# Four column tiles of a projection as seven half-size products, and the looks at an output matrix moved one stage earlier

## The chip, the cores and the metric

The kernel runs on one core of one Trainium2 chip. The metric is the device time of one execution in microseconds; lower is better. The time before is 679.76 us, the median of 3 runs (679.46 to 680.37). The engines are named as in the profile: PE multiplies matrices, PEld loads its stationary operand, ACT applies functions and copies, DVE does elementwise work, POOL helps a little, and SP issues nearly all transfers from one queue.

## The reference

Two branches read the same `x` (2048 positions, 1024 channels) and are mixed by a gate per position:

```python
g = sigmoid((x * gate_w).sum(-1, keepdims=True))
# branch A: attention over a window of 8 positions, 2 apart, 32 heads of 32
qkv = x @ wqkv;  o = window_attention(q, k, v);  a = o @ wo
# branch B: a gated MLP that mixes positions
z  = gelu(x @ w_in)                       # 2048 x 3584
z1 = z[..., :1792];  z2 = layernorm(z[..., 1792:])
gm = w_sp @ z2 + b_sp[:, None]            # 2048 x 2048 times 2048 x 1792
b  = (z1 * gm) @ w_out
out = g * a + (1 - g) * b
```

Inputs and output are bf16; sums are kept in float32.

## The kernel before

The work on PE goes in stages, one after another. The order on every engine is the order in which the program writes it.

1. z2, first column group (512 columns of `x @ w_in`), positions on the partitions.
2. The projection `x @ wqkv`, in chunks of four blocks of 128 columns. The last two chunks are done as "row pairs" (`row_pair`, line 636): two rows of blocks by two columns of blocks by two halves of the 1024 channels, with seven products in place of eight. This needs sums of blocks of x (`x_sums`, `a22s`, held in z2's later place) and sums of blocks of the weights (`t_w`, `t3_w`). To keep the 16-bit sums accurate, x and the weights are scaled by a power of two first (`whole_power`, line 496), and the results are scaled back when they leave PSUM.
3. z2, the remaining columns: group 1 for positions blocks 2 to 15 (14 tiles), then groups 2 and 3 for all 16 blocks (`z2_tile`, line 291). ACT applies gelu and keeps a sum; after every block of groups 2 and 3 it also squares the whole row of 1792 for the variance (line 760).
4. z1: 14 column tiles of 128 columns (f = 0 to 13), four products of 512 positions each (loop at line 798). ACT applies gelu; the tiles go to a scratch tensor `z1_d`.
5. The spatial product with `w_sp`: two chunks plainly (`g_chunk`, line 822), the other two as seven products (`seven_products`, line 922).
6. The output: w_out and wo, in pairs of rows (`mix_pair`, `both_pairs`, line 1129).

The window attention runs on DVE meanwhile, from stage 2 into stage 5, as a list of steps (`attention_steps`, line 419). ACT does its exponential (line 381) and, when two groups of heads are stored, eight abs-sums of 512 columns (line 415).

A planner places the side work. `Beat` (line 230) holds a clock `beat.now` that advances by 1/2360 us for each column that PE is given. `beat.at(t, fn)` writes `fn` into the program as soon as the clock has passed `t`; attention steps are written when their planned start on DVE is less than `lead` ahead (3 us, in the row pairs 1 us with the large steps halved, `fine`). The clock decides the place of an instruction in its queue, not when it runs: each queue runs in order as its waits allow.

All results of PE go through one pool of PSUM tiles with eight slots (line 79): a product must wait when all eight hold results that nobody has read yet.

Behind the row pairs SP gets a fixed list of loads: w_in for groups 2 and 3 of z2 (line 746), the column of gate_w into the same buffer (line 747), a part of z2 kept aside (line 748), w_in for z1 (`load_w1`, line 488), and a part of the bias (line 752).

Before w_out and wo are multiplied as sums, their largest absolute values are needed. These "looks" (loop at line 773) load two blocks of 128 rows at a time (512 KB) into one of two slots, and ACT sums the absolute values (line 779): seven looks for w_out, four for wo, one every 7 us in stage 4, the sum 11 us behind its load in the planner's clock.

## Time and profile before

| | us |
|---|---|
| median of 3 runs | 679.76 |
| the profiled execution | 679.49 |
| its span | 677.7 |
| PE busy | 673.0 |
| DVE busy | 558.4 |
| ACT busy | 415.8 |
| the projection ends, z2's stretch begins | 196.28 |
| z2 ends, z1 begins | 262.45 |
| z1 ends, g_chunk begins | 359.14 |
| seven_products begins | 455.83 |
| last product of PE begins | 673.23 |

The granted TensorE clock was 1.00 of full speed. In the profile a row of the timeline gives start, duration, engine, line and operation, and in brackets how long the engine had been idle before it and what released it. "SPq" is SP's queue of transfers, where a row's start is the time of issue. The chain of waits names, step by step, the work that set the end.

### The profile page before, as it was taken

The page shows a single profiled execution, that of the slowest core. Times are in us where ns is not written, and L with a number is a line of the kernel's source. Part 1 is how long each engine was busy: PE and PEld are TensorE (multiplying, and loading weights), DVE is VectorE, ACT ScalarE, POOL GpSimd, SP SyncE. Part 2 cuts the span into 40 slices and gives each one's busy share as a digit, 9 for nine tenths or more (in the row PEclk, how much of TensorE's full clock was granted, in tenths as well). Part 3 has the DMA queues.
Part 4 walks back from the last instruction along what each step waited for, and adds up shares of the span by engine and source line. Part 5 has one row for each costly group of instructions (what it writes and reads, how often), then busy time and mean ns, then how long its engine had stood idle before and what let it go on. Part 6 is the DMA issues. An engine that isn't in the chain of part 4 may idle for free.

```text
span 677.7 us, 8946 instructions
## 1 busy us (share of the span) xinstructions
PE 673.0 (99%) x3311; PEld 355.1 (52%) x3311; DVE 558.4 (82%) x667; ACT 415.8 (61%) x765; POOL 29.4 (4%) x62
## 2 busy tenths in 40 slices
PE   9999999999999999999999999999999999999997
PEld 4499666666654555444444444444444444444443
DVE  4769779999999999999999889974578888766653
ACT  4369676655584999775765996437877542332332
POOL 1000010000000032000010001000000001000000
PEclk9999999999999999999999999999999999999999
DMA  9992977636667416799879997036211513222210
GB/s 231 194 167 61 223 179 224 152 71 175 167 159 213 150 61 164 156 266 350 281 254 227 267 218 183 0 94 233 78 50 44 156 37 88 65 69 68 65 45 32
DMA packets 183192, 100.28 MB, mean 148 GB/s; under 512 B 143342, under 2 KB 169708, under 8 KB 182892
## 3 DMA queue, kind: packets, MB, share of 16 engines
q1 hardware_dynamic: 182316, 97.61, 55.6%
q10 hardware_dynamic: 576, 2.10, 1.0%
q8 instruction: 26, 0.43, 0.3%
q14 instruction: 18, 0.15, 0.1%
q0 software_dynamic: 256, 0.00, 0.0%
HBM read 55.91 MB, written 29.16 MB: 126 GB/s over the span
## 4 chain that ended last, share of the span: by engine, by line
PE 99%; DMA 1%; SPq 0%; ACT 0%; DVE 0%; issue 0%; DVEq 0%
PE ps L621 16%; PE ps L300 14%; PE ps L836 14%; PE ps L809 14%; PE ps L1038 12%; PE ps L910 12%; PE ps L644 7%; PE ps L1127 6%; PE ps L1117 1%; DMA arena<-in_B_w_in_dram 1%; SPq L514 0%; ACT arena L1181 0%; DVE arena L1107 0%; DVEq L1314 0%
## 5 line engine op out<-in xcount | busy, mean ns | idle before, releaser
L621 PE MATMUL ps<-arena 128*128 128x512 bf16 (+1 forms) x640 | 115.1, 336 | 0.0
L300 PE MATMUL ps<-arena 128*128 128x512 bf16 (+1 forms) x512 | 97.9, 353 | 0.5 <-DMA arena<-in_B_w_in_dram 0.5
L621 PEld LDWEIGHTS <-arena 128*128 128x128 bf16 x640 | 83.4, 144 | 27.7
L836 PE MATMUL ps<-arena 128*128 128x512 bf16 x448 | 96.9, 379 | 0.0
L809 PE MATMUL ps<-arena 128*128 128x512 bf16 x448 | 96.9, 379 | 0.0
L1038 PE MATMUL ps<-arena 128*128 128x512 f16 (+1 forms) x392 | 92.8, 379 | 0.0
L910 PE MATMUL ps<-arena 128*128 128x512 bf16 (+1 forms) x392 | 84.8, 379 | 0.0
L300 PEld LDWEIGHTS <-arena 128*128 128x128 bf16 x512 | 50.1, 98 | 47.7 <-DVE arena L320 0.6
L836 PEld LDWEIGHTS <-arena 128*128 128x128 bf16 x448 | 43.9, 98 | 52.8
L809 PEld LDWEIGHTS <-arena 128*128 128x128 bf16 x448 | 43.8, 98 | 52.6
L351 DVE TENSOR_TENSOR arena<-arena 128x8192 bf16<-128x8192 bf16 (+1 forms) x20 | 71.1, 3567 | 0.3
L394 DVE TENSOR_TENSOR arena<-arena,att_A 128x8192 bf16<-128x8192 bf16 (+1 forms) x20 | 71.2, 3564 | 0.0
L1038 PEld LDWEIGHTS <-arena 128*128 128x128 f16 (+1 forms) x392 | 38.4, 98 | 46.2
L910 PEld LDWEIGHTS <-arena 128*128 128x128 bf16 (+1 forms) x392 | 38.3, 98 | 46.3
L354 DVE TENSOR_TENSOR arena<-arena 128x4096 bf16<-128x4096 bf16 (+1 forms) x32 | 56.2, 1756 | 0.8
L305 ACT ACTIVATE arena<-ps 128x512 bf16<-128x512 f32 x64 | 34.2, 536 | 31.2 <-PE ps L300 31.2
L644 PE MATMUL ps<-arena 128*128 128x512 f16 (+1 forms) x224 | 52.4, 379 | 0.0
L630 ACT CAST arena<-ps 128x512 bf16<-128x512 f32 (+1 forms) x64 | 33.1, 561 | 28.4 <-PE ps L621 28.4
L1127 PE MATMUL ps<-arena 128*128 128x512 f16 (+3 forms) x200 | 50.3, 375 | 0.0
L1107 DVE SCALAR_TENSOR_TENSOR arena<-ps,g_s,arena 128x512 bf16<-128x512 f32 (+2 forms) x33 | 24.0, 733 | 29.5 <-ACT arena L1159 20.0
L644 PEld LDWEIGHTS <-arena 128*128 128x128 f16 (+1 forms) x224 | 32.2, 144 | 16.1
L812 ACT ACTIVATE arena<-ps 128x512 bf16<-128x512 f32 x56 | 30.8, 595 | 10.6 <-PE ps L809 10.2
(187 smaller groups left out, 785.4 us busy)
## 6 DMA issues: line engine op xcount, KB each, us to landing
arena<-v_d SPq DMA_DIRECT2D x8, 960.0 KB, 5.1
arena<-k_d SPq DMA_DIRECT2D x7, 960.0 KB, 5.9
arena<-in_A_wqkv_dram SPq DMA_DIRECT2D x24, 256.0 KB, 4.4
z_d<-arena SPq DMA_DIRECT2D x12, 512.0 KB, 8.8
o_d<-arena SPq DMA_DIRECT2D x4, 1024.0 KB
arena<-in_B_w_in_dram SPq DMA_DIRECT2D x4, 1024.0 KB, 9.0
arena<-z_d SPq DMA_DIRECT2D x15, 256.0 KB, 4.8
out_dram<-arena SPq DMA_DIRECT2D x15, 256.0 KB, 2.2
```

The lines of the kernel that those rows point to most:

```text
L300: nc.tensor.matmul(ps[:, 0:N], xT[:, kt, i * P:(i + 1) * P], w2[c][:, kt, 0:N], start=(kt == 0), stop=(kt == KT - 1))
L305: nc.scalar.activation(z2[:, 4 * c:4 * c + n // P, i, :], ps[:, 0:n].rearrange("p (f q) -> p f q", q=P), ACT.Gelu_apprx_tanh, accum_out=s1 ...
L351: TT(prod.rearrange("p (w j c) -> p w j c", w=W, j=8, c=C)[:, w0:w1], in0, in1, ALU.mult)
L354: return lambda: TT(pv[:, :, 0:half], pv[:, :, 0:half], pv[:, :, half:2 * half], ALU.add)
L394: TT(prod.rearrange("p (w j d h) -> p w j d h", w=W, j=8, d=DH, h=HG)[:, w0:w1], in0, in1, ALU.mult)
L621: nc.tensor.matmul(ps[:, n0:n1].rearrange("p (t c) -> p t c", c=C), lhsT, wgt[:, pos0:pos1, kt, :], start=(kt == 0), stop=(kt == KT - 1))
L644: nc.tensor.matmul(dst[:].rearrange("p (t c) -> p t c", c=C), lhs(k), rhs[:, :, k, :], start=first and k == 0, stop=k == 3, skip_group_che ...
L809: nc.tensor.matmul(ps[:], w1[:, kt, (f % 4) * P:(f % 4 + 1) * P], xT[:, kt, 512 * c:512 * (c + 1)], start=(kt == 0), stop=(kt == KT - 1))
L836: nc.tensor.matmul(ps[:], z2[:, f, i, :], wsp[:, i, :, :].rearrange("p a t -> p (a t)"), start=False, stop=(i == 15), skip_group_check=True)
L910: nc.tensor.matmul(dst[:], lhs[:, k, :], rhs(k), start=False, stop=k == 7, skip_group_check=True)
L1038: nc.tensor.matmul(dst[:], lhs[:, j, :], rhs(j), start=first and j == 0, stop=j == 6, skip_group_check=not first)
L1127: nc.tensor.matmul(dst, lhs[:, k, :], rhs[:, k, :], start=first and k == 0, stop=k == 3, skip_group_check=not first)
```

## The change

The first four column tiles of z1 (512 columns of w_in) leave stage 4. They are computed right behind the row pairs, from the sums of x that are still there, in four sets (`ZSet`): each set is one pair of column tiles by 512 positions of even and 512 of odd number, seven products of four matmuls each. The weights are the stationary operand here, x and its sums the moving one; in products one and four x is read at every second element. Each set copies partial results between PSUM tiles on ACT, adds on DVE, applies gelu on ACT with every second element written, and the second set of each column pair stores two tiles to `z1_d`. z1's loop now runs over f = 4 to 13.

What goes with it:

- The 512 columns of w_in are loaded during the projection into the place of group 1 of z2's weights (`z_w`); ACT takes their absolute sums and scales them, DVE forms four sums of weights. z2's group 1 is therefore loaded a second time, and groups 1 and 2 change places.
- The staging of the row pairs goes from four pairs of buffers to three.
- The tile of group 1 for position block 2 is computed inside the last set.
- Behind the sets SP's list is: w1 of chunk 2, w2 of groups 2 and 3, gate_w's column, the part of z2, the bias. w1 of chunk 0 is no longer loaded; chunks 1 and 3 come later.
- Four of the eleven looks move into z2's stretch, into the place of `z_w`, each as two transfers of 256 KB, the first due at once and its abs-sum 9 us later, one every 5.5 us; the sum is written in place. The other seven stay in z1's stage, 7 us apart.
- `scale_sp(2)` moves from DVE to ACT; the load of w_out's first part and the scalings and sums of w_out are moved some places later in `seven_products`.
- In the last pair of rows the final 512 columns are split 256 and 256 in place of 384 and 128, and ACT's scaling ahead of it is split in two.

```diff
+    z_w = w2[1]
+    z_w16 = reg(CD_OFF, KT * 2 * ZC).bitcast(F16).rearrange("p (k c) -> p k c", k=KT)
+    t_z = [z_w16[:, 4:8, 0:256], z_w16[:, 4:8, 256:512],
+           reg(CD_OFF + 16384, 1024).bitcast(F16).rearrange("p (k c) -> p k c", k=4), z_w16[:, 0:4, 768:1024]]
+    odd_f32 = [reg(off, 1024).bitcast(F32) for off in (CD_OFF + 17408, EF_OFF + 14336)]
+    z1p_slots = [reg(off, 4096).rearrange("p (f t) -> p f t", f=2) for off in (EF_OFF + 8192, EF_OFF + 4096)]
...
+    first_looks = [w2_01[:, 4 * r:4 * r + 4, ZC:2 * ZC] for r in range(2)]
...
+    class ZSet:
+        def __init__(self, n):
+            self.r, self.v = divmod(n, 2)
+            self.e5, self.odd = e5_f32[self.v], odd_f32[self.v]
+
+        def mm(self, dst, w, x, first):
+            w = w[:, :, 128 * self.r:128 * self.r + 128]
+            for k in range(4):
+                nc.tensor.matmul(dst[:], w[:, k, :], x[:, k, 512 * self.v:512 * self.v + 512],
+                                 start=first and k == 0, stop=k == 3, skip_group_check=not first)
+            beat.run(4 * 512)
+
+        def bank(self):
+            return psum.tile([P, 512], F32, name="ps", tag="ps")
+
+        def gelu(self, h, odd, src, by):
+            t0 = 1024 * self.v + odd
+            nc.scalar.activation(z1p_slots[self.r][:, h, t0:t0 + 1023:2], src, ACT.Gelu_apprx_tanh, scale=by)
+
+        def one(self):
+            self.pa = self.bank()
+            self.mm(self.pa, z11, x_block(0, 0), True)
+            self.pb = self.bank()
+            nc.scalar.activation(self.pb[:], self.pa[:], ACT.Copy, scale=x_by)
+
+        def two(self):
+            pe = self.bank()
+            self.mm(pe, t_z[0], x_sums[0], True)
+            nc.scalar.activation(self.e5, pe[:], ACT.Copy, scale=z_backs[:, 1:2])
+
+        def three(self):
+            self.mm(self.pb, t_z[1], x_sums[1], False)
+            self.pc = self.bank()
+            nc.scalar.copy(self.pc[:], self.pb[:])
+
+        def four(self):
+            self.mm(self.pa, z21, x_block(1, 0), False)
+            self.gelu(0, 0, self.pa[:], z_backs[:, 0:1])
+
+        def five(self):
+            self.mm(self.pb, t_z[3], x_sums[2], False)
+            self.pd = self.bank()
+            nc.scalar.copy(self.pd[:], self.pb[:])
+            nc.vector.scalar_tensor_tensor(self.odd, self.pb[:], z_backs[:, 1:2], self.e5, ALU.mult, ALU.add)
+            beat.on_vector(0.75)
+
+        def six(self):
+            self.mm(self.pc, z22, x_sums[3], False)
+            nc.vector.scalar_tensor_tensor(self.e5, self.pc[:], z_backs[:, 1:2], self.e5, ALU.mult, ALU.add)
+            beat.on_vector(0.75)
+
+        def seven(self):
+            self.mm(self.pd, t_z[2], a22s, False)
+            self.gelu(0, 1, self.pd[:], z_backs[:, 1:2])
+
+        def rest(self):
+            self.gelu(1, 1, self.odd, 1.0)
+            self.gelu(1, 0, self.e5, 1.0)
+            if self.v:
+                for h in range(2):
+                    f = self.r + 2 * h
+                    sync.dma_start(z1_d[:, :, f * 512:(f + 1) * 512].rearrange("c p t -> p c t"),
+                                   z1p_slots[self.r][:, h, :].rearrange("p (c t) -> p c t", c=4))
...
+    load_w2(1)
+    z_sum(3)
+    for z in z_sets[0:1]:
+        z.two()
+        z.three()
+        z.four()
+    send()
+    for z, z_next in zip(z_sets, z_sets[1:]):
+        z.five()
+        z_next.one()
+        z_next.two()
+        z.six()
+        z_next.three()
+        z.seven()
+        z_next.four()
+        z.rest()
+    z_sets[3].five()
+    ps_2 = psum.tile([P, 512], F32, name="ps", tag="ps")
+    for kt in range(KT):
+        z2_mm(ps_2, 2, 1, kt, ZC)
+    beat.run(KT * ZC)
+    z_sets[3].six()
+    z_sets[3].seven()
+    z_sets[3].rest()
     beat.lead = LEAD
     beat.fine = False
-    for c in (2, 3):
-        sync.dma_start(w2[c][:, :, 0:ZW[c]], win_v[:, :, FH + ZC * c:FH + ZC * c + ZW[c]])
+    load_w1(2)
+    load_w2(2)
+    load_w2(3)
     sync.dma_start(w2[3][:, :, 256:257], gw_v)
     sync.dma_start(z2[:, 4:8, 0:2, :], z2_d[:])
-
-    load_w1(0)
-    load_w1(1)
     sync.dma_start(b_in[:], bass.AP(tensor=B_b_sp.tensor, offset=B_b_sp.offset + 1024, ap=[[1, P], [P, 8]]))
-    for i in range(2, 16):
+
+    wout_v = B_w_out.rearrange("(f p) n -> p f n", p=P)
+    wo_rows = A_wo.rearrange("(k p) n -> p k n", p=P)
+
+    def look(k, t, slot):
+        src = wout_v[:, 2 * k:2 * k + 2, :] if k < 7 else wo_rows[:, 2 * k - 14:2 * k - 12, :]
+        total = w_l1[:, k:k + 1] if k < 7 else wo_l1[:, k - 7:k - 6]
+        for f in range(2):
+            beat.at(t, lambda f=f: sync.dma_start(slot[:, 2 * f:2 * f + 2, :], src[:, f, :].rearrange("p (h c) -> p h c", h=2)))
+        beat.at(t + 9.0, lambda: nc.scalar.activation(slot, slot, ACT.Abs, accum_out=total))
+
+    for k in range(4):
+        look(k, beat.now - 1.0 + 5.5 * k, first_looks[k % 2])
+    for g in range(NG):
+        beat.at(beat.now + 5.0 + 7.0 * g, lambda g=g: turn_wo(g))
+    z2_out(ps_2, 2, 1)
+    for i in range(3, 16):
         z2_tile(i, 1)
-        if i == 3:
-            send()
+        if i == 8:
+            load_w1(1)
...
-    for k in range(11):
-        slot = look_slots[k % 2]
-        src = wout_v[:, 2 * k:2 * k + 2, :] if k < 7 else wo_rows[:, 2 * k - 14:2 * k - 12, :]
-        total = w_l1[:, k:k + 1] if k < 7 else wo_l1[:, k - 7:k - 6]
-        beat.at(beat.now + 2.0 + 7.0 * k, lambda src=src, slot=slot: sync.dma_start(
-            slot.rearrange("p (f n) -> p f n", f=2), src))
-        beat.at(beat.now + 13.0 + 7.0 * k, lambda total=total, slot=slot: nc.scalar.activation(
-            look_out, slot, ACT.Abs, accum_out=total))
...
+    for k in range(4, 11):
+        look(k, beat.now + 2.0 + 7.0 * (k - 4), look_slots[k % 2])
...
-    for f in range(NF):
+    for f in range(4, NF):
```

93 lines of the change are left out of this document (64 added, 29 removed).

## Prediction

> **What bounds the kernel now.** I read the page's parts on engines and on the chain that ended last first, then the chain in order of time.
>
> ```profile
> span 677.7 us, 8946 instructions
> PE 673.0 (99%) x3311; PEld 355.1 (52%) x3311; DVE 558.4 (82%) x667; ACT 415.8 (61%) x765; POOL 29.4 (4%) x62
> ...
> PE 99%; DMA 1%; SPq 0%; ACT 0%; DVE 0%; issue 0%; DVEq 0%
> ...
> 195.42 0.86 PE ps L644 x4
> 196.28 66.16 PE ps L300 x368
> 262.45 96.69 PE ps L809 x448
> ```
>
> PE is busy 673.0 of 677.7 us and is 99% of the chain: the end is set by the number of products. The chain's steps join without a gap: z2's 368 matmuls end at 262.44, where z1's begin, and z1 takes 96.69/448 = 0.216 us for a matmul of 512 columns. A matmul taken away is worth 0.216 us, as long as PE keeps having a free PSUM slot and its operands. So the second reading is of ACT, which empties PSUM in the stretch that the change fills.
>
> ```profile
> 220.50:262.40 41.90, 41.90 (x257) 25.04 (x256) 39.81 (x45) 40.80 (x100) 8.69 (x7) 1.00 0.29 99
> 255.98 0.58 ACT L305 ACTIVATE arena<-ps 128x512 bf16<-128x512 f32 x1
> 257.05 1.70 ACT L760 ACTIVATE arena<-arena 128x1792 bf16<-128x1792 bf16 x1
> 258.74 0.58 ACT L305 ACTIVATE arena<-ps 128x512 bf16<-128x512 f32 x1
> 267.03 0.58 ACT L305 ACTIVATE arena<-ps 128x512 bf16<-128x512 f32 x1
> ```
>
> The row by stage gives ACT 40.80 of 41.90 us in z2's groups 2 and 3, and the timeline of ACT shows it saturated: one block (two gelus and the square) takes 258.74 - 255.98 = 2.76 us, while PE needs 512 + 257 columns x 8 = 2.62 us for it. ACT falls back; the last block's first gelu begins at 267.03, 5.5 us after its product. Eight slots cover that (seven further tiles are 9.2 us), so nothing is lost today. But ACT has no room there.
>
> **The change, term by term.** The sum starts from the profiled execution's own 679.49 us (0.27 below the median; 1.8 us of it lie outside the span).
>
> *Products.* Four column tiles cost 4 x 4 x 8 = 128 matmuls; four sets cost 4 x 7 x 4 = 112. 16 x 0.216 = -3.46 us. z2's tiles stay 14 in number. Bounds on the pace:
>
> ```profile
> L621 PEld LDWEIGHTS <-arena 128*128 128x128 bf16 x640 | 83.4, 144 | 27.7
> L300 PEld LDWEIGHTS <-arena 128*128 128x128 bf16 x512 | 50.1, 98 | 47.7 <-DVE arena L320 0.6
> ```
>
> The only strided operands on PE today are stationary: the projection's weight load with a stride of 16 elements takes 144 ns, a contiguous one 98, +46 ns for 128 columns, and both hide behind 216 ns. The sets read x at every second element as moving operand in 4 x 8 = 32 matmuls. If that cost what the wide stride costs, 4 x 46 = 0.18 us each, it would be +5.9 us; at the other end nothing. I take nothing, since a stride of two is nearer to contiguous than to sixteen. The Trainium skill, "SBUF — State Buffer", section "Door 1: The DMA port swizzle (why `[64,N]` ≈ `[32,N]`)", says that SBUF is read by lines of 16 bytes and that strides are free while several hits fall on a line; two-byte elements at every second place give four hits, so by it the price is nothing, and the 144 ns rows, where each element has its own line, agree with it.
>
> *The sets themselves.* A set is 28 matmuls, 6.05 us of PE, and holds eight ACT operations.
>
> ```profile
> L415 ACT ACTIVATE arena<-arena 128x512 bf16<-128x512 bf16 x32 | 20.0, 624 | 0.1
> L662 ACT ACTIVATE ps<-ps,x_up 128x512 f32<-128x512 f32 x8 | 5.3, 660 | 0.9 <-PE ps L644 0.3
> L556 ACT ACTIVATE arena<-arena,x_up 128x4096 bf16<-128x4096 bf16 x1 | 3.7, 3722 | 0.0
> 193.05 1.73 PE ps L644 x8
> 197.22 0.74 DVE L677 SCALAR_TENSOR_TENSOR arena<-ps,u_l,arena 128x512 bf16<-128x512 f32 x1
> 197.88 0.74 DVE L680 SCALAR_TENSOR_TENSOR arena<-ps,u_l,arena 128x512 bf16<-128x512 f32 x1
> ```
>
> Until the copy for which set 1's third product waits, ACT has eight operations at about 0.6 each (a copy from PSUM is 0.66), the gelu table's load (1.28, a row below) and about four abs-sums of stored attention (0.62): 8.1 to 8.6 us against nine products, 7.8 us. That is a wait of 0.3 to 0.8 us. Later sets hang on DVE: a gelu waits for an addition there, and behind it on ACT's queue stands the copy for the next set but one. In the row pairs the last such product ended at 193.05 + 1.73 = 194.78 and its addition began at 197.88, 3.1 us late; 3.1 + 0.74 + gelu 0.6 + two copies 1.2 = 5.6 us fit into the 6.05 us there are. The gelus write every second element, which no row shows; reading so costs ACT nothing (L556, 3722 ns for 4096 elements, the pace of its contiguous rows), and I take the same for writing. Were it twice the time, 16 x 0.6 = 9.6 us more of ACT in 24 us that are four fifths full already would cost PE up to some 5 us. Together +0.6 us, between 0 and 5.
>
> *The weights' preparation* (1 MB loaded, four abs-sums and four scalings of 1024 on ACT, a small chain on DVE and POOL) lies beside the projection and is due 25 us later: 0. The second load of group 1 (1 MB) has the sets' 25 us as cover: 0; without the cover it would cost about 9 us. Staging with three pairs leaves a pair's stores two pairs, 15 us, to land: 0; were they late, ACT's and DVE's writes would wait first.
>
> *SP's queue behind the sets.* This is the term that decides. T is the end of the last set: 195.42 plus 124 matmuls, 222.2 us.
>
> ```profile
> 198.23 1.17 SPq L746 DMA_DIRECT2D arena<-in_B_w_in_dram  x2
> 206.78 0.37 SPq L747 DMA_DIRECT2D arena<-in_gate_w_dram  x1
> 207.86 1.35 SPq L488 DMA_DIRECT2D arena<-in_B_w_in_dram  x2
> 210.92 4.06 SPq L602 DMA_DIRECT2D k_d<-arena  x1
> ...
> SPq L747 <- DMA arena<-in_B_w_in_dram: 7.3, 1, 7.3
> ```
>
> SP issues in order, and the gate column (L747) waits for the landing of the load before it into the same buffer: 7.3 us today, 206.78 - 198.23 = 8.6 us behind the issue of 1.5 MB. The looks stand behind this wait in the changed order. What is ahead: the last store of z1 waits for a gelu that waits for DVE (3.1 + 0.74 + 0.6 behind the sixth product, which ends 0.9 before T), so it goes out at about T + 4; then w1 and w2, in all 0.5 + 1 + 1 + 0.5 MB.
>
> ```profile
> 198.00:202.00 4.00, 4.00 (x21) 1.81 (x19) 3.96 (x3) 3.56 (x11) 0.00 (x0) 1.00 0.99 205
> 207.90:213.00 5.10, 5.10 (x26) 2.30 (x24) 5.07 (x2) 2.06 (x6) 0.00 (x0) 1.00 0.91 266
> ...
> arena<-in_A_wqkv_dram SPq DMA_DIRECT2D x24, 256.0 KB, 4.4
> ```
>
> While such loads ran, 205 and 266 GB/s were moved; at the mean of 235, 3.15 million bytes take 13.4 us: the gate column is released at about T + 18. Then 210.92 - 206.78 - 1.35 = 2.8 us of issues (column, z2's part, bias), and 4.4 us for a transfer of 256 KB to land: the first look's data arrive at X = T + 25. (Ends: 21, with the higher rate and an early store; 29, at the 8.6 us per 1.5 MB.) The Trainium skill, "DMA: Bandwidth & Descriptors", section "Measured (HBM→SBUF, 128 partitions, SWDGE, issued from GpSimd)", gives 6.15 us for 1 MB; by it 3 MB take 9.2 us and X would be about T + 21, an estimate from that page which the 8.6 us for 1.5 MB here do not support.
>
> *ACT behind the first look.* Its abs-sum is due at T + 8, behind the fifth tile, and in ACT's queue every later gelu stands behind it.
>
> ```profile
> L779 ACT ACTIVATE arena<-arena 128x2048 bf16<-128x2048 bf16 x11 | 21.0, 1911 | 13.8 <-DMA arena<-in_B_w_out_dram 8.8 <-DMA arena<-in_A_wo_dram 5.1
> 220.50 0.60 ACT L305 ACTIVATE arena<-ps 128x512 bf16<-128x512 f32 x1 [1.04 <-PE ps L300]
> 222.93 1.28 ACT L381 ACT_TABLE_LOAD   x1
> 224.22 0.63 ACT L381 ACTIVATE att_L<-att_L 128x512 f32<-128x512 f32 x1
> 224.87 1.28 ACT L305 ACT_TABLE_LOAD   x1
> ```
>
> Looks do wait for data: 13.8 us over eleven today, with 11 us of lead, and PE does not notice. The four moved looks are eight issues on SP, about 0.4 us each, and the loads behind them in the queue (wo's turning, w1 of chunk 1, the attention's v) wait with them for the slots; those are used much later: 0. Here ACT stands from T + 9 to X. PE fills the eight slots by 13 x 1.73 = T + 22.5 and stops. From X on, ACT has before it, until it frees the slot of z2's last tile: four looks at 1.89 (start to next start), eight gelus at 0.58, the exponential with two table loads 3.2, eleven blocks at 2.76 and two gelus 1.06: 46.8 us. With the last tile's 0.87 z2 ends at X + 47.7 against a plan of 13 x 1.73 + 16 x 2.62 = T + 64.4; z1's first tile waits another 1.5 for the next square. The wait is X - T - 15.2 = +9.8 us (ends 5.8 and 13.8).
>
> *DVE behind that.* The exponential is due at T + 7.5 to T + 9.2 (222 today, plus 8 additions of 0.75, four sums of 0.7 and a little, in the planner's clock), so more likely behind the look than ahead of it. Then DVE, ready for it at about T + 12.5, idles until X + 4.4: 17 us, of which PE's own lateness gives back 10.
>
> ```profile
> 359.10:407.50 48.40, 48.40 (x226) 21.94 (x224) 42.16 (x44) 41.16 (x82) 0.38 (x4) 1.00 1.04 244
> 407.50:455.80 48.30, 48.30 (x225) 21.91 (x224) 43.67 (x64) 22.98 (x34) 2.25 (x4) 1.00 0.40 97
> 204.44 0.69 DVE L357 TENSOR_TENSOR arena<-arena 128x1024 bf16<-128x1024 bf16 x1
> 454.15 2.29 DVE L887 TENSOR_TENSOR arena<-arena 128x4096 f16<-128x4096 bf16 x1 [0.69 <-PE ps L836]
> L871 DVE TENSOR_SCALAR arena<-arena,s_up 128x2048 bf16<-128x2048 bf16 x4 | 2.9, 746 | 0.0
> ```
>
> DVE idles 6.2 + 4.6 = 10.8 us in the stage of g_chunk today. The change adds eight additions (0.66 from start to start, 5.3), four sums (0.69, 2.8), a chain of about 1.3, takes 2.9 away (scale_sp), and PE comes 2.9 earlier: 1.4 us are left. Seven us late, DVE is 5.6 late for the first of the seven products, where the third product needs the sum of L887 at 455.83 + 3.46 = 459.3; that sum is ready at 456.4 today, 2.9 to spare: +2.7, I take +2.5 (0 to 6). In seven_products the moved loads and scalings cost nothing if DVE is on time.
>
> *The tail.*
>
> ```profile
> 673.23 1.04 PE L1127 MATMUL ps<-arena 128*128 128x384 f16 x8
> 673.43 0.69 ACT L1181 ACTIVATE arena<-ps,omg 128x512 f32<-128x512 f32 x1 [2.79 <-PE ps L1038]
> 674.15 0.88 DVE L1107 SCALAR_TENSOR_TENSOR arena<-ps,g_s,arena 128x384 bf16<-128x384 f32 x2 [1.48 <-ACT arena L1181]
> ```
>
> After PE's last long product come ACT 0.69 and two additions 0.88. Split in halves, the first addition starts after half the scaling: about -0.2 us (0 to -0.3). The looks left in z1's stage, 7 x 1.89 in 69 us, hide; `scale_sp(2)` on ACT falls where ACT is half idle.
>
> Sum: 679.49 - 3.46 + 0.6 + 9.8 + 2.5 - 0.2 = 688.7 us.
>
> **The rivals.**
>
> *The looks arrive in time (faster).* Place: the landing of the first look. Its wait is X - T - 15.2, and the change breaks even at 3.1 us of it, X = T + 18.3; below T + 15 nothing is left and the time is 679.49 - 3.46 + 0.6 - 0.2 = 676.4 us. For it: the gate column's wait could end sooner if the loads overlap better than at 198 to 207, and the abs-sum's 9 us of lead would do if the look were issued at T. Against it: the wait of 7.3 us stands in the trace, and 3 MB lie ahead in place of 1.5. Chance 0.19; another 0.05 for X near the break-even, no measurable change.
>
> *The exponential stands ahead of the look.* Then DVE does not idle, 3.2 us fall out of ACT's list behind X, and the time is 679.49 - 3.46 + 0.6 + 6.6 - 0.2 = 683.0 us. Its due time overlaps the look's for a third of its span: chance 0.22.
>
> *The products are not cheaper.* If the stride of two costs 5.9 us and the looks are in time: 676.4 + 5.9 = 682.3 us. No row shows it; chance 0.04.
>
> **How the numbers follow.** The forecast has 0.50; slower by over 0.2% (1.4 us, about what a measurement of this kernel can tell from no change) has 0.50 + 0.22 + 0.04 = 0.76, within 0.2% 0.05, faster 0.19. The forecast alone reaches from 683 (X at T + 21, DVE on time) to 693 (X at T + 29). The range also takes in the exponential's rival and reaches into the faster case: 677 to 693 leaves out about two thirds of that case and a few hundredths above.
>
> **What would show it.** Right: no gap on PE until about T + 22; the gate column's issue some 12 us behind the load before it; ACT idle before its first look for over 10 us, released by a transfer; PE waiting on ACT in z2's stretch for about 10 us in all; DVE waiting for the exponential. z2 and the sets together end near 296 in place of 286. Wrong: the first look landing before T + 15, PE's chain without gaps through z2, a matmul pace other than 0.216 us in the sets, or DVE late at seven_products without an idle stretch before.

## The result: 699.2 us, and the profile after

The changed kernel takes 699.18 us (median of 4, 697.51 to 702.49), the kernel before on the same chip 679.81 (4, 679.46 to 680.37): ratio 1.029, 95% interval 1.025 to 1.033. The forecast was 688.7 with a range of 677 to 693. The direction was right; the loss, 19.4 us, is about twice the one forecast, and the time lies outside the range. One execution of the kernel before, 1020.06 us at a granted clock of 0.655, was in a slower state and is left out of all ratios.

The profiled execution took 699.96 us. The head of the changed kernel's page (busy time, share of the span, instructions):

```profile
span 698.1 us, 8950 instructions
PE 676.4 (97%) x3244; PEld 355.0 (51%) x3295; DVE 564.3 (81%) x684; ACT 439.0 (63%) x796; POOL 26.5 (4%) x64
```

PE does 16 matmuls less and is busy 3.4 us longer. (The 16 show in the weight loads, 3311 and 3295; the count of matmuls falls by more because some of their records are missing.) So PE doesn't only wait, it also runs slower somewhere. The waits of PE in the changed kernel (engine and line <- what ended the wait: us in all, times, longest):

```profile
PE ps L309 <- ACT arena L314: 6.8, 3, 2.9
PE ps L681 <- ACT ps L699: 5.0, 1, 5.0
PE ps L309 <- ACT gl_s L318: 1.9, 1, 1.9
PE ps L1055 <- DVE arena L1032: 0.6, 1, 0.6
```

L681 is the row pairs, L309 z2, L1055 `seven_products`. Two places, then, and the forecast knew only the second. The chain of waits (start, us, step) gives the stages' bounds, to be read beside 134.12, 196.28, 262.45 and 359.14 of before:

```profile
134.16 0.88 PE ps L681 x4
230.65 3.47 PE ps L309 x16
309.51 7.75 PE ps L958 x35
378.78 3.24 PE ps L985 x15
```

By stage, with the row pairs' end at 204.74 less the first set's four matmuls (0.87), and T, the end of the last set, at 230.65:

| term | forecast | in the profiled execution | worked out |
|---|---|---|---|
| 16 products less | -3.46 | -3.46 | 112 in place of 128 x 0.2163 |
| the weights' preparation beside the projection | 0 | +7.6 | row pairs 134.16 to 203.87 in place of 62.16 |
| the sets themselves | +0.6 | +0.8 | 204.74 to 230.65, less 116 x 0.2163 |
| z2 behind the first look | +9.8 | +14.4 | 230.65 to 309.51, less the planned 64.4 |
| DVE at `seven_products` | +2.5 | +0.6 | the wait above |
| the tail | -0.2 | 0.0 | last product to the end of the span: 4.47 both times |

The sum is +19.9; 20.5 were measured in this execution (699.96 - 679.49).

**The first place: ACT behind a late factor.** The timelines of ACT and DVE in the changed kernel, ahead of the row pairs:

```profile
126.67 1.60 ACT L667 CAST arena<-ps 128x512 bf16<-128x512 f32 x3
134.20 1.15 ACT L606 ACTIVATE arena<-arena,z_up 128x1024 bf16<-128x1024 bf16 x1 [5.93 <-DVE z_up L514]
128.78 1.22 DVE L588 TENSOR_TENSOR arena<-arena 128x2048 f16<-128x2048 bf16 x1
134.01 0.15 DVE L514 TENSOR_SCALAR z_up<-z_up 128x1 int32<-128x1 int32 x1
```

The first scaling of z_w (L606) waits 5.93 us for `z_up`, and the copies that empty PSUM stand behind it on ACT. DVE makes `z_up` in 0.15 us, but only at 134.01, behind the four sums of q's weights (L588 to L594, 1.22 us each), which stand ahead in its queue. PE then waits for a copy at the first row pair.

**The second place: the looks.** SP's and ACT's timelines in z2's stretch:

```profile
233.85 3.31 SPq L863 DMA_DIRECT2D arena<-in_B_w_in_dram  x2
244.64 0.37 SPq L894 DMA_DIRECT2D arena<-in_gate_w_dram  x1
246.43 3.54 SPq L905 DMA_DIRECT2D arena<-in_B_w_out_dram  x4
258.74 1.47 SPq L905 DMA_DIRECT2D arena<-in_B_w_out_dram  x2
241.32 0.63 ACT L390 ACTIVATE att_L<-att_L 128x512 f32<-128x512 f32 x1
251.66 1.91 ACT L906 ACTIVATE arena<-arena 128x2048 bf16<-128x2048 bf16 x1 [9.72 <-DMA arena<-in_B_w_out_dram]
268.96 1.91 ACT L906 ACTIVATE arena<-arena 128x2048 bf16<-128x2048 bf16 x1 [4.48 <-DMA arena<-in_B_w_out_dram]
```

The gate column's issue (L894) comes 10.8 us behind the load before it, as forecast, and the first look's abs-sum (L906) starts at 251.66 = T + 21.0, the early end of the forecast's 21 to 29. The exponential (L390) ran ahead of it, as in the second rival. But there is a second wait that the forecast didn't have: the fourth look, issued at 258.74, lands 10 us later, and ACT waits 4.48 us for it. A third hold-up comes near the end of z2: ACT's next exponential, which the kernel before has in z1's stage (at 272.49), stands there from 298.07 to 301.30 with its two table loads of 1.28 us. ACT is still behind then, and PE's last two gaps, 1.89 and 1.29 us, fall there.

**The clock.** The matmuls behind a wait are slow. First PE's timeline in z2 behind its gaps, then PE's busy time in some steps of 2 us (stretch, length, PE busy, matmuls, granted clock, DMA share, GB/s):

```profile
255.72 14.68 PE L309 MATMUL ps<-arena 128*128 128x512 bf16 x79 [2.62 <-ACT arena L314]
273.27 26.72 PE L309 MATMUL ps<-arena 128*128 128x512 bf16 x149 [2.87 <-ACT arena L314]
301.88 1.06 PE L309 MATMUL ps<-arena 128*128 128x257 bf16 x8 [1.89 <-ACT gl_s L318]
```

```profile
140.00:142.00 2.00, 0.51 (x2) 0.50 0.94 353
146.00:148.00 2.00, 2.00 (x11) 1.00 0.00 0
254.00:256.00 2.00, 0.28 (x1) 0.79 0.57 165
256.00:258.00 2.00, 2.00 (x6) 0.50 0.88 278
274.00:276.00 2.00, 1.95 (x13) 1.00 0.26 104
304.00:306.00 2.00, 1.56 (x4) 0.50 0.00 0
```

Behind the wait of 5.03 us PE gets half its clock until 145.94, behind one of 2.62 us (253.1 to 255.7) until 258.6, behind the last two until 309.8; behind one of 2.87 us (270.4 to 273.3) the clock stays at 1.00. In all the clock is at 0.50 for 17.1 us, and by this working about 6 us of the loss come from that: in the row pairs half of 141.49 to 145.94, 2.2 us, in z2 half of 255.72 to 258.58 and of 304.22 to 309.51, 4.1 us. So z2's 14.4 us are 8.9 us of idle time, 4.1 of clock and 1.4 in which PE goes at ACT's pace, 2.76 us a block.

### The profile page after: what moved, and what is told of

Read it like the earlier page. It is cut to its first block, busy times and chain, and to the rows that moved or that the text cites. A ratio compares the mean times of both kernels' runs of the same rounds, so it can differ in the third digit from the quotient of the medians.

```text
span 698.1 us, 8950 instructions
## 1 busy us (share of the span) xinstructions
PE 676.4 (97%) x3244; PEld 355.0 (51%) x3295; DVE 564.3 (81%) x684; ACT 439.0 (63%) x796; POOL 26.5 (4%) x64
## 4 chain that ended last, share of the span: by engine, by line
PE 73%; DVE 10%; ACT 9%; DMA 4%; issue 2%; SPq 1%; another core or an unknown queue 0%; ACTq 0%; DVEq 0%
PE ps L658 16%; PE ps L1183 12%; PE ps L1055 12%; PE ps L958 10%; PE ps L681 7%; PE ps L1272 6%; PE ps L309 6%; PE ps L734 3%; ACT arena L920 3%; DVE arena L403 2%; DMA arena<-in_B_w_in_dram 2%; PE ps L985 2%; DMA arena<-in_B_w_out_dram 2%; ACT arena L314 2%; DVE arena L409 1%
## 5 line engine op out<-in xcount | busy, mean ns | idle before, releaser
L658 PE MATMUL ps<-arena 128*128 128x512 bf16 (+1 forms) x637 | 115.4, 337 | 0.2
L309 PE MATMUL ps<-arena 128*128 128x512 bf16 (+1 forms) x501 | 103.6, 362 | 9.5 <-ACT arena L314 6.8
L658 PEld LDWEIGHTS <-arena 128*128 128x128 bf16 x640 | 83.6, 145 | 28.4 <-issue 1.0
L985 PE MATMUL ps<-arena 128*128 128x512 bf16 x439 | 96.4, 379 | 0.5
L1183 PE MATMUL ps<-arena 128*128 128x512 f16 (+1 forms) x382 | 91.3, 379 | 0.4
L1055 PE MATMUL ps<-arena 128*128 128x512 f16 (+1 forms) x385 | 84.6, 379 | 0.9 <-DVE arena L1032 0.6
L309 PEld LDWEIGHTS <-arena 128*128 128x128 bf16 x512 | 51.2, 100 | 60.9 <-issue 15.7
L985 PEld LDWEIGHTS <-arena 128*128 128x128 bf16 x448 | 43.8, 98 | 52.9
L958 PE MATMUL ps<-arena 128*128 128x512 bf16 x314 | 69.2, 380 | 0.3
L1055 PEld LDWEIGHTS <-arena 128*128 128x128 bf16 (+1 forms) x392 | 38.3, 98 | 47.1 <-DVE arena L1032 1.1
L681 PE MATMUL ps<-arena 128*128 128x512 f16 (+1 forms) x224 | 54.1, 388 | 5.0 <-ACT ps L699 5.0
L958 PEld LDWEIGHTS <-arena 128*128 128x128 bf16 x320 | 31.4, 98 | 37.8 <-issue 0.3
L1272 PE MATMUL ps<-arena 128*128 128x512 f16 (+2 forms) x199 | 50.1, 375 | 0.2
L314 ACT ACTIVATE arena<-ps 128x512 bf16<-128x512 f32 x64 | 34.0, 539 | 22.3 <-PE ps L309 22.2
L1252 DVE SCALAR_TENSOR_TENSOR arena<-ps,g_s,arena 128x512 bf16<-128x512 f32 (+1 forms) x33 | 24.0, 733 | 29.3 <-ACT arena L1304 20.0
L681 PEld LDWEIGHTS <-arena 128*128 128x128 f16 (+1 forms) x224 | 32.4, 145 | 22.7 <-issue 7.2
L667 ACT CAST arena<-ps 128x512 bf16<-128x512 f32 (+1 forms) x64 | 32.6, 558 | 15.2 <-PE ps L658 14.1
L409 DVE TENSOR_TENSOR arena<-arena 128x4096 bf16<-128x4096 bf16 x16 | 36.6, 2286 | 0.2
```

The costliest lines, as they stand in the source:

```text
L309: nc.tensor.matmul(ps[:, 0:N], xT[:, kt, i * P:(i + 1) * P], w2[c][:, kt, 0:N], start=(kt == 0), stop=(kt == KT - 1))
L314: nc.scalar.activation(z2[:, 4 * c:4 * c + n // P, i, :], ps[:, 0:n].rearrange("p (f q) -> p f q", q=P), ACT.Gelu_apprx_tanh, accum_out=s1 ...
L658: nc.tensor.matmul(ps[:, n0:n1].rearrange("p (t c) -> p t c", c=C), lhsT, wgt[:, pos0:pos1, kt, :], start=(kt == 0), stop=(kt == KT - 1))
L681: nc.tensor.matmul(dst[:].rearrange("p (t c) -> p t c", c=C), lhs(k), rhs[:, :, k, :], start=first and k == 0, stop=k == 3, skip_group_che ...
L958: nc.tensor.matmul(ps[:], w1[:, kt, (f % 4) * P:(f % 4 + 1) * P], xT[:, kt, 512 * c:512 * (c + 1)], start=(kt == 0), stop=(kt == KT - 1))
L985: nc.tensor.matmul(ps[:], z2[:, f, i, :], wsp[:, i, :, :].rearrange("p a t -> p (a t)"), start=False, stop=(i == 15), skip_group_check=True)
```

## The experiments

Ratios are to the kernel before, on the same chip, with 95% intervals.

| run | us | ratio |
|---|---|---|
| the changed kernel | 699.2 | 1.029 [1.025, 1.033] |
| chain first | 693.6 | 1.021 [1.018, 1.024] |
| looks first | 697.4 | 1.026 [1.024, 1.027] |
| both | 694.9 | 1.022 [1.019, 1.024] |
| looks back | 682.1 | 1.003 [1.002, 1.004] |
| both, wo turned later | 689.0 | 1.013 [1.011, 1.014] |
| looks back, z_w later | 688.9 | 1.014 [1.011, 1.018] |
| both, wo and w1 later | 683.0 | 1.005 [1.003, 1.007] |
| all repairs | 680.2 | 1.0014 [1.0002, 1.0026] |
| all repairs, wo closer | 681.3 | 1.0025 [1.0015, 1.0036] |
| all repairs, exponential first | 680.0 | 1.0000 [0.9991, 1.0009] |
| before, exponential first | 679.7 | 0.9998 [0.9989, 1.0007] |

### The chain ahead of the sums

```diff
         if j == 15:
+            next(z_steps)
+            next(z_steps)
             for k in range(4):
                 q_sum(k)
...
-        if j in (0, 2):
-            next(z_steps)
         if 3 <= j < 7:
             z_scale(j - 3)
```

> Only the order on DVE differs from the changed kernel: the six small operations that make z_up and its inverse stand ahead of the four weight sums of 1.22 us (q_sum) instead of behind them. Theory 1 (ACT stood in its queue behind a scaling whose factor was late on DVE): z_up is ready at about 129.2 instead of 134.0, ACT's first scaling waits about 1 us instead of 5.9, PE's wait of 5.0 us at the first row pair falls below 0.7, and the stretch at clock 0.50 behind it (139.2 to 145.9, 2.4 us of PE) is gone too: 699.2 - 7.4 = 691.8 us, 690.5 to 693. Rival (it is the volume of ACT, four abs-sums and four scalings, some 9 us, and not the order): PE still waits 3 us or more there, 696 to 699.

693.56 us (692.3 to 696.81). Its timeline of ACT and its waits of PE:

```profile
128.78 1.15 ACT L606 ACTIVATE arena<-arena,z_up 128x1024 bf16<-128x1024 bf16 x1 [1.06 <-DVE z_up L514]
PE ps L681 <- ACT ps L706: 1.5, 1, 1.5
PE ps L681 <- ACT ps L699: 0.7, 1, 0.7
PE ps L681 <- DVE arena L714: 0.4, 1, 0.4
```

The wait for `z_up` falls from 5.93 to 1.06 us, as expected, PE's wait at the first row pair goes with it, and so does the slow clock there. 5.6 us come back in the median, not 7.4: PE still waits 2.6 us in all in the row pairs, 1.9 of them because DVE's additions (L714) come late, 0.7 because a store of q had not landed when its buffer was wanted again. The sets end at 226.25 in place of 230.65. So the order on DVE is shown to be the cause of more than half of the first loss; a lateness of DVE is left.

### The first two looks ahead of w2

`look_load` issues the two transfers of a look.

```diff
+    for k in range(2):
+        look_load(k, first_looks[k])
-    load_w1(2)
     load_w2(2)
     load_w2(3)
...
     sync.dma_start(b_in[:], ...)
+    load_w1(2)
...
-        look(k, beat.now - 1.0 + 5.5 * k, first_looks[k % 2])
+        look(k, beat.now - 1.0 + 5.5 * k, first_looks[k % 2], loaded=k < 2)
```

> Only SP's order behind the sets differs from the changed kernel: the loads of the first two looks go out ahead of w2 of groups 2 and 3, and w1 of chunk 2 goes behind the bias. Theory 1 (ACT stood behind an abs-sum whose data were late): the first look lands some 5 us behind its issue, by about T + 8 (T is the end of the last set), ACT's wait of 9.7 us is gone, PE's waits in z2's stretch (8.9 us of idle time in all and 5.3 us lost at clock 0.50) fall to 0 to 3 us: 699.2 - 12.5 = 686.7 us, 685 to 689. Rival (ACT has no room for four looks in z2's stretch, whenever their data come: two gelus and a square take 2.76 us there and PE needs 2.62): most of PE's waits stay, 692 to 699.

697.41 us (696.17 to 698.58): the time that the rival gave. Its timeline of ACT:

```profile
240.47 1.89 ACT L912 ACTIVATE arena<-arena 128x2048 bf16<-128x2048 bf16 x1
257.57 1.91 ACT L912 ACTIVATE arena<-arena 128x2048 bf16<-128x2048 bf16 x1 [8.32 <-DMA arena<-in_B_w_out_dram]
266.47 1.91 ACT L912 ACTIVATE arena<-arena 128x2048 bf16<-128x2048 bf16 x1 [4.75 <-DMA arena<-in_B_w_out_dram]
```

Looks 0 and 1 no longer wait, and the third and fourth now wait 8.32 and 4.75 us. Theory 1 in its plain form falls: with the first look on time, later ones are late. Look 2 was issued only at 248.60, since the gate column's wait (until 244.53) stood ahead of it on SP's queue, and then took 9 us. Nor is it the rival's reason, since ACT isn't short of time here; it stands idle for 13 us.

### Both

The two edits in one kernel.

> Both edits together, the order on DVE and SP's order. Theory 1 (two waits that have nothing to do with each other): the gains add, 699.2 - 7.4 - 12.5 = 679.3 us, 677 to 682, so at the time of the kernel before, or a little under it. Rival (one lateness is handed on: a stretch that starts earlier waits longer for the same attention or the same transfer): under two thirds of the sum, 685 or more.

694.9 us (691.94 to 695.81), no better than the chain alone: the rival's side, and again because the wait moves on. Look 2 was issued at 244.68 and read at 253.20, look 3 at 251.81 and at 262.06. Ahead of them or between them SP had issued w1 of chunks 2 and 1 (1 MB each) and transfers that turn wo.

### All looks back in z1's stage

On top of the chain's edit:

```diff
-    for k in range(4):
-        look(k, beat.now - 1.0 + 5.5 * k, first_looks[k % 2])
...
-    for k in range(4, 11):
-        look(k, beat.now + 2.0 + 7.0 * (k - 4), look_slots[k % 2])
+    for k in range(11):
+        look(k, beat.now + 2.0 + 6.0 * k, look_slots[k % 2])
...
-    beat.at(beat.now + 45.0, ...
+    beat.at(beat.now + 53.0, ...
```

The last pair of lines moves the maximum of w_out's sums, which needs the looks.

> The order on DVE as in the run with the chain ahead of the sums, and all eleven looks in z1's stage, one every 6 us, as the kernel before had them (there every 7 us). SP's list behind the sets is that of the changed kernel, so the gate column still waits for its landing. Theory 1: nothing on ACT stands behind a late transfer in z2's stretch, which takes 64 to 66 us behind the last set instead of 78.9: 699.2 - 7.4 - 14 = 677.8 us, 676 to 680, and the sets by themselves make the kernel about 2 us faster than before. Rival (the loads behind the sets, 3 MB in place of 1.5 MB, are late for z2's products, with or without looks): PE waits for a transfer in z2's stretch, 683 or more.

682.11 us (681.18 to 682.59). The last looks are loaded over a part of z1's tiles that stands there for `g_chunk` already, so the output is not the reference's; the amount of work is the same. Its timeline of PE:

```profile
226.91 64.60 PE L309 MATMUL ps<-arena 128*128 128x512 bf16 x360
291.35 39.01 PE L956 MATMUL ps<-arena 128*128 128x512 bf16 x180
```

z2 runs without a gap, 226.91 to 291.35 = 64.4 us, exactly as planned, with the gate column, w1 and w2 loaded as in the changed kernel. So z2's products were never late for their own loads; all 11.5 us between this run and the chain alone are the looks' doing. Of the 4.3 us over the expected 677.8, 3.3 stand ahead: waits of PE in the row pairs.

### wo turned later, then w1 later

```diff
-    for g in range(NG):
-        beat.at(beat.now + 5.0 + 7.0 * g, lambda g=g: turn_wo(g))
...
+    for g in range(NG):
+        beat.at(beat.now + 6.0 + 10.0 * g, lambda g=g: turn_wo(g))
     w_steps = whole_power(w_up, omg[:])
```

> As the run with both edits, and the eight transfers that turn wo go back into z1's stage, where the kernel before had them. There look 2 landed 8.5 us after its issue and look 3 some 10 us (ACT waited 6.6 and 4.7 us for them), with wo's turning and w1 (2 MB) in flight beside them. Theory 2 (the late data only moved from the first look to the third and fourth, because transfers written beside them share the way): without wo's turning they land some 5 us behind their issue, ACT's two waits fall from 11.3 us to below 5 in sum, PE waits at most 2 us in z2's stretch: 694.9 - 6 = 689 us, 686 to 691. Rival (ACT's volume: two gelus and a square at 2.76 us a block, so looks cost their own time wherever their data are): no change, 692.5 to 696.

688.97 us (687.62 to 691.73), as expected, but the reason holds by half only: in the profiled execution, the slowest of the four, ACT still waits 6.23 and 2.51 us for looks 2 and 3, not under 5 in all, and they are read 8.4 and 9.6 us behind their issue. Two loads of w1 are still issued ahead of and between these looks. The next run takes them away too:

```diff
-    load_w1(2)
...
-        if i == 8:
-            load_w1(1)
     for i in range(16):
         for c in range(2, 4):
             z2_tile(i, c)
+        if i in (4, 8):
+            load_w1(i // 4)
```

> As the run with wo turned later, and w1 of chunks 1 and 2 (2 MB) go out behind the looks, in the second half of z2's stretch. Theory 2: looks 2 and 3 then share the way with nothing but the gate column's wait ahead of look 2; ACT waits for them at most 3 us in sum, no wait of PE is left but for the exponential's table loads near the end (0.6 to 3 us): 685 us, 682.5 to 687. Rival (ACT's volume): 690 or more, like the run before it.

682.98 us (680.05 to 687.1). The timelines of ACT and PE:

```profile
248.84 1.91 ACT L911 ACTIVATE arena<-arena 128x2048 bf16<-128x2048 bf16 x1 [1.57 <-DMA arena<-in_B_w_out_dram]
227.14 64.60 PE L309 MATMUL ps<-arena 128*128 128x512 bf16 x360
```

One wait of 1.57 us is left on ACT, and PE goes through z2 in 64.4 us with all four looks in it. Theory 2 holds: the transfers issued beside the looks made them late, in two ways. Look 2 went out at nearly the same time as with both edits (244.07 and 244.68) and was read 4.8 us behind its issue in place of 8.5; look 3 went out at 246.01 in place of 251.81, because fewer issues stood ahead of it on SP. The rival, that ACT has no room for four looks there, is refuted, and with it the forecast's worry over ACT's 2.76 us per block.

### z_w loaded later

```diff
-    sync.dma_start(z_w, win_v[:, :, 0:512])
     for j in range(NJ):
+        if j == 12:
+            sync.dma_start(z_w, win_v[:, :, 0:512])
...
-        look(k, beat.now + 2.0 + 6.0 * k, look_slots[k % 2])
+        look(k, beat.now + 2.0 + 4.3 * k, look_slots[k % 2])
...
```

> As the run with all looks in z1's stage, but one look every 4.3 us, so that the last is read before z1's first part is loaded into the same place (in the run with 6 us between them the last looks overwrote a part of it; its time stands, its output does not), and the load of z_w (1 MB) goes out 12 rows later in the projection's second chunk. Theory 1b (this load ahead of the attention's transfers makes ACT wait 2.5 us for the next v, the exponential comes 2.6 us later and DVE stays late by that into the row pairs, where PE waited 3.3 us in all): the first copy of v waits no more, DVE's exponential step is back at 89 us, PE's waits in the row pairs fall to about 1 us: 682.1 - 2.5 = 679.6 us, 678.5 to 680.5. Rival (DVE is late because of its own added work, six small operations and three sums, 3.4 us): 681.3 to 682.5.

688.88 us (685.88 to 695.58), slower than the looks back alone. Two things happened at once, and the trace parts them. The changed kernel's exponential step on DVE, then this run's and what PE did in z1's stage:

```profile
91.69 0.43 DVE L381 TENSOR_TENSOR att_m<-att_L 128x256 f32<-128x256 f32 x1 [11.10 <-ACT att_L L390]
```

```profile
89.10 0.42 DVE L381 TENSOR_TENSOR att_m<-att_L 128x256 f32<-128x256 f32 x1 [8.29 <-ACT att_L L390]
288.60 43.33 PE L957 MATMUL ps<-arena 128*128 128x512 bf16 x200
PE ps L957 <- ACT arena L960: 4.2, 4, 2.1
```

With z_w's load out of the way the exponential comes 2.6 us earlier, PE waits 0.8 us in the row pairs in place of 3.3, and z1 begins at 288.60 in place of 291.35: theory 1b holds for the row pairs, but not its time of 679.6 us. With eleven looks at 4.3 us PE waits 4.2 us for ACT in z1's stage, and 2.2 us for DVE at `seven_products`; that the looks stand too close there is the likely reason, and no run varies it alone.

### All repairs

The edits of chain first, looks first, wo later, w1 later and z_w later in one kernel.

> The changed kernel with all repairs that held: the six small operations ahead of the weight sums on DVE, the first two looks' loads ahead of w2, w1 of chunks 1 and 2 behind the looks, wo turned in z1's stage, and z_w's load 12 rows later. The waits have different causes, so the last one's gain (row pairs and sets ended 2.75 us earlier with z_w's load later) should come on top of the 683.0 of the run with w1 later: 680.2 us, 679.0 to 681.5, no difference from the kernel before that can be told. Rival (DVE's list of attention steps is the next bound, an earlier PE waits for it at seven_products): 681.5 to 683.

680.18 us (679.33 to 682.98), ratio 1.0014 [1.0002, 1.0026]. All waits of PE over 0.3 us:

```profile
PE ps L1061 <- DVE arena L1038: 1.1, 1, 1.1
PE ps L681 <- ACT ps L699: 0.9, 1, 0.9
```

(A third, 0.8 us at the start, stands in every run, the kernel before included.) So 19.0 of the 19.4 us are undone by five moves of instructions within their queues, without a change to a single product. That shows that it isn't the sets and their sums by themselves that made the kernel slower, but where the work beside them stood. The 3.46 us that the products save by count are not won: the kernel comes out within 0.3% of the one before.

### wo closer

`6.0 + 7.0 * g` in place of `6.0 + 10.0 * g`.

> As the run with all repairs, with wo turned every 7 us in place of every 10, so that the last of its eight transfers is out before the spatial weights of the second chunk are loaded, for which PE waited 0.9 us in the run with w1 later. Theory: that wait goes, 0.5 to 0.9 us less than the run with all repairs. Rival: the transfers of z1's stage (looks, spatial weights of the first chunk) come closer together and ACT's looks wait instead: the same time or up to 2 us more.

681.32 us (679.67 to 683.27): the rival's side, though the two intervals of the ratio overlap (1.0015 to 1.0036 and 1.0002 to 1.0026). The wait of 0.9 us was gone already in the run with all repairs, and PE waits 0.7 us for ACT in z1's stage.

### The stride of two

```diff
-            self.mm(self.pa, z11, x_block(0, 0), True)
+            self.mm(self.pa, z11, xT[:, 0:4, 0:1024], True)
...
-            self.mm(self.pa, z21, x_block(1, 0), False)
+            self.mm(self.pa, z21, xT[:, 4:8, 0:1024], False)
...
-            t0 = 1024 * self.v + odd
-            nc.scalar.activation(z1p_slots[self.r][:, h, t0:t0 + 1023:2], ...)
+            t0 = 1024 * self.v + 512 * odd
+            nc.scalar.activation(z1p_slots[self.r][:, h, t0:t0 + 512], ...)
```

> As the run with all repairs, with the stride of two taken out of the sets: products one and four read 512 neighbouring elements of x and the gelus write 512 neighbouring elements, so the sets multiply other positions and the first four tiles of z1 are not the reference's; the work is of the same size. The 100 products of the sets from the row pairs' end to z2's tile took 22.45 us with the stride, 0.82 more than 100 x 0.2163. Theory (reading every second element costs PE nothing): 22.3 to 22.5 again. Rival (the 28 strided ones among them cost 0.03 us each): 21.65. For the gelus' writing, which took ACT 0.84 us from PSUM and 0.68 from SBUF: 0.57 to 0.60 if the stride is what costs, unchanged if it is the 32-bit input. The time of the whole moves by less than 1 us either way.

679.62 us, one execution. The groups of the sets' gelus, with the stride (all repairs) and without:

```profile
L743 ACT ACTIVATE arena<-ps,u_l 128x512 bf16<-128x512 f32 x8 | 6.6, 839 | 2.5 <-PE ps L734 2.3
L743 ACT ACTIVATE arena<-arena 128x512 bf16<-128x512 f32 x8 | 5.5, 765 | 0.0
```

```profile
L743 ACT ACTIVATE arena<-ps,u_l 128x512 bf16<-128x512 f32 x8 | 5.4, 687 | 3.1 <-PE ps L734 3.0
L743 ACT ACTIVATE arena<-arena 128x512 bf16<-128x512 f32 x8 | 4.5, 618 | 0.0
```

Writing every second element costs ACT 0.15 us per gelu, 2.4 us over the sixteen; it was counted as nothing, and PE's list of waits with the stride has none in the sets. On PE the 100 matmuls take 198.09 to 220.54 = 22.45 us with the stride, and 199.19 to 221.35 = 22.16 without: 0.29 us over 28 strided ones, 0.01 us each. The durations of single matmuls (least, median and greatest, in ns), with the stride and without, agree:

```profile
L734 PE MATMUL ps<-arena x109: 376/379/390, 196.3 to 223.8; 128*128 128x512 f16 x64, 128*128 128x512 bf16 x45
L734 PE MATMUL ps<-arena x109: 376/379/379, 197.5 to 224.6; 128*128 128x512 f16 x64, 128*128 128x512 bf16 x45
```

Neither side of the expectation is met: both runs keep some 0.5 us over 100 x 0.2163 in this stretch that the stride doesn't explain, and the stride costs a third of what the rival gave. The rival "the products are not cheaper", with 0.18 us each, is out. By the rule of the Trainium skill, "SBUF — State Buffer", section "Door 1: The DMA port swizzle (why `[64,N]` ≈ `[32,N]`)", that the prediction drew on, the reading would cost nothing; measured are 0.01 us on 0.216.

### Gaps of known length

```diff
             if c == 0 and f in (2, 5, 8, 11):
+                for n in {2: (2048,) * 8 + (1024,), 5: (2048,) * 9, 8: (2048,) * 8, 11: (2048,) * 10}[f]:
+                    nc.scalar.activation(look_out[:, 0:n], look_out[:, 0:n], ACT.Abs)
```

> The kernel before, with ACT held up four times in z1's stage by 8.5, 9, 8 and 10 extra abs operations of 2048 elements (about 16.1, 17.1, 15.2 and 19.0 us) on a buffer that nobody reads, at the column tiles 2, 5, 8 and 11. PE runs out of free slots after about 13.8 us and then idles some 2.5, 3.5, 1.6 and 5.4 us. If the granted clock follows the share of idle time in fixed stretches of 3.41 us (in the changed kernel it changed at 139.18, 145.9, 255.16, 258.6, 302.95 and 309.77, all on one such grid), it falls to 0.50 behind every stretch that is idle for more than about half, for 3.4 or 6.8 us, and the changes lie on one grid again; the gaps of 3.5 and 5.4 always lower it, those of 1.6 and 2.5 by where they fall. Rival (only a gap longer than a whole stretch lowers it): only the longest gap, perhaps that of 3.5, is followed by a slower clock. The time itself rises by the gaps and the slow stretches, 13 us for the gaps and up to 7 for the clock.

724.22 us, one execution, 35.7 us of it in the four gaps. These became longer than meant, 6.38, 8.98, 9.91 and 10.39 us, probably since ACT had its looks to do as well. So this run can't tell short gaps, but it shows the grid. Five of the eight steps of 0.1 us in which the clock changed (stretch, length, PE busy, matmuls, granted clock):

```profile
294.50:294.60 0.10, 0.00 (x0) 0.62 1.16 353
301.30:301.40 0.10, 0.10 (x2) 0.74 0.00 0
325.20:325.30 0.10, 0.00 (x0) 0.72 0.18 77
355.90:356.00 0.10, 0.00 (x0) 0.82 0.00 0
366.20:366.30 0.10, 0.10 (x1) 0.97 0.00 0
```

Read to the share of the step, the clock falls at 294.52, 325.24 and 355.96, 30.72 us = 9 x 3.413 apart, and comes back after 6.83 = 2 x 3.413 and 10.24 = 3 x 3.413. In the changed kernel the changes are at 139.12, 145.94, 255.17, 258.58, 302.96 and 309.78: again whole multiples of 3.413. The Trainium skill, "TensorE: Matmul & The Clock Gate", section "Part 1: The HAM clock gate (the "warmup" mystery)", describes a free-running window of 4096 cycles at 1.2 GHz, 3413 ns, and a clock at half or full by how busy PE has been; these traces agree to the hundredth. Its section "HAM oscillation — how this bites in real kernels" puts the bound at idle gaps of more than about 3.4 us, and there the traces differ: a gap of 2.62 us, and gaps of 1.89 and 1.29 us one after the other, were each followed by half the clock in the changed kernel. What fits the traces better is the idle share of one window, as near as the modelled ends of matmuls give it: 61% and more came ahead of a lower clock in every case here, 55% did once (1.89 us in the window before 302.96) and once not (the same gap in the run with the chain first), 54% (1.84 of the 2.87 us) did not. That the share decides is read from these cases; no run set it on purpose.

### The exponential first

The guess for what is left in the repaired kernel is DVE's lateness. In the projection's second chunk DVE waits 8.2 us for an exponential that stands behind two copies of v on ACT.

```diff
-        if j in (6, 9):
+        if j in (6, 11):
             v_order(5 if j == 6 else 2)
```

> As the run with all repairs, and in the projection's second chunk the two copies of v (3.8 us on ACT) go out two rows later, so that the attention's exponential stands ahead of them: DVE waited 8.2 us for it in the run with all repairs. Theory (what is left of the loss, PE's waits of 0.9 us in the row pairs and 1.1 us at seven_products, is DVE's lateness): DVE goes on some 3.8 us earlier from 85 us on, both waits go: 680.2 - 2.0 = 678.2 us, 677.4 to 679.2, faster than the kernel before by 0.2%. Rival (the next transfer of q and k, or ACT, takes the exponential's place as what DVE waits for): 679.7 to 680.7, no difference.

> The kernel before with that same edit alone. PE has no wait there that DVE could end, so nothing is to gain: 679.8 us, within 0.2%. If it gets faster all the same, the gain of the other run isn't the sets' 16 products, but the exponential's place.

680.03 us (11 executions, 678.68 to 681.29) and, for the kernel before with this edit, 679.66 (679.53 to 680.4): neither differs from the kernel before. That is the rival's range; the theory's, 677.4 to 679.2, is missed. PE's waits in the repaired kernel shrink, but don't go:

```profile
PE ps L681 <- ACT ps L699: 0.7, 1, 0.7
PE ps L1061 <- DVE arena L1038: 0.6, 1, 0.6
```

DVE has its exponential 3.4 us earlier (85.40 in place of 88.84), then waits 0.85 us for a sum of ACT (until 93.17) and 2.04 for a transfer of v (until 109.97), waits that the run with all repairs doesn't have: the next transfer took the exponential's place, as the rival said. The profiled execution is the fastest of the eleven, 678.68 us, 1.24 under that of the edited kernel before (679.92). By its trace 3.46 - 0.8 (sets) - 0.7 - 0.6 = 1.4 of the products' gain are left. The median doesn't show them. By the medians no version here beats the kernel before; where the other executions lose that microsecond is open.

## Why the prediction came out too low

Right were the step on SP's queue, the wait on the gate column, and the first look at T + 21, at the early end (z1's last store went out at T + 0.9, 3 us earlier than worked out); the eight slots that hide ACT's wait at first (PE's first gap began at 253.1, T + 22.4, where T + 22.5 was worked out); the sets' own cost (0.6 against 0.8, though 0.3 of it are the stride, which was counted as nothing); and that slower was the likeliest.

Luck was in the 9.8 us for z2. With the look's real time, X = T + 21, the prediction's own formula X - T - 15.2 gives 5.8 us; a late X hid a part of what was missing. Add the wait for the fourth look, 4.5 us, and the slow clock, 4.1 us, and the measured 14.4 us are there.

What failed, by its own steps:

- *"The weights' preparation ... lies beside the projection and is due 25 us later: 0."* The largest miss against its price, 7.6 us (5.0 of waiting, 2.2 of slow clock). The prediction counted the time that this work takes and not its place in the queues. Four scalings on ACT wait for a chain on DVE. The program writes the chain six tiles of 1.73 us ahead of the row pairs (134.16), so at about 123.8; DVE came to it at 133.64, and 4.9 of these 10 us are sums that stood ahead in the same queue. The run with the chain first shows it. The 1 MB of z_w, priced at 0 as well, delayed ACT's copy of v by 2.5 us and with it DVE by 2.6 (z_w later).
- *"The loads behind them in the queue ... wait with them for the slots ... 0."* They delay the looks among them, by their issues on SP and in flight. The list of what ACT has behind X counted four looks at 1.89 us each, with their data there; the fourth (look 3) landed 10 us behind its issue, and ACT waited 4.5 us for it. The runs with wo and w1 later show it.
- *A wait costs its length.* The prediction takes that for granted without a word. PE ran at half clock behind three of its gaps, about 6 us in all.
- *"DVE behind that", +2.5.* The exponential went ahead of the look, a case that had 0.22; PE waited 0.6 us for DVE at the end.
- *"Staging with three pairs ... 0", the tail -0.2.* Misses of less than a microsecond: in the chain-first run ACT waits 2.9 us for a store of q to land, PE 0.7 of it (no run has four pairs again); the tail gave nothing.

The rival "the exponential stands ahead of the look" had the order right and 683.0 us, and missed for the same two reasons. The rival "the looks arrive in time", 676.4 us, describes the kernel with all repairs, which needs 680.2; PE's waits of 0.9 and 1.1 us are a part of that difference, the rest is open.

Two sums of the prediction don't come out. Its low end of 683 for "X at T + 21, DVE on time" is 682.2 by its own terms (676.4 + 5.8). And its estimate from the Trainium skill, "DMA: Bandwidth & Descriptors", section "Measured (HBM→SBUF, 128 partitions, SWDGE, issued from GpSimd)", doesn't follow from the 6.15 us for 1 MB that it names: three times that is 18.5 us, not 9.2. That X was T + 21 in the trace is no support for it; nothing in the sum rests on it.

## What to carry to other kernels

Side work in idle time is free only if nothing in its queue depends on an engine that lags behind the plan: follow every operand back to the queue that makes it, and read that engine's real place at that time from the trace, not the planner's. When loads move, look at what is in flight beside them, not only at what is ahead of them; here the order of a few issues was worth 10 us, and the products saved 3.5 by count. And price a gap of PE of about 2 us and more with the slow clock that may follow: up to half of the next 3.4 or 6.8 us.

## What the runs showed of the hardware that I had not expected

- The TensorE clock changed on a fixed grid of 3.413 us; a window that was idle for 61% or more was followed by at least one at half clock, with matmuls of 512 columns at 0.43 us in place of 0.216. The same pair of gaps, 1.89 and 1.29 us at the end of z2, came ahead of a lower clock in the changed kernel and not in the run with the chain first. They lay differently on the grid, but the first took 55% of its window both times, so what decided is open.
- A load of 512 KB took 4.8 us from its issue until ACT could read it with little else in flight (244.07 to 248.84, look 2 with wo and w1 later), and 8.5 to 10.3 us with 2 MB of w1 and the turning of wo beside it (244.68 to 253.20 and 251.81 to 262.06, both edits). Without wo's turning it was 8.4 and 9.6 us (245.20 to 253.57 and 250.68 to 260.23, wo later), so w1 seems to be the larger part.
- The changed kernel and its variants spread over 1.4 to 9.7 us from one execution to the next, the kernel before over 0.6 to 1.7. The clock's grid can make equal gaps cost differently, but the run with wo and w1 later varies by 7 us and its trace has no gap over 1.6 us; what does it is open.
- ACT writing every second bf16 element: 0.84 in place of 0.69 us for 512 elements from PSUM. PE reading every second: 0.01 us more per matmul of 0.216.
